# Up products of the last tile's last three MLP chunks in the first attention units, with the w2 splits placed by their use

## The chip, the cores and the metric

The kernel runs on one core of a Trainium2 chip. The metric is the time of one execution on the device in microseconds (us); less is better. A profile is one execution recorded by the hardware profiler: the engines are PE (matrix products; PEld are its weight loads), DVE (vector), ACT (activation), POOL (GpSimd) and SP, which here only issues DMAs.

## The reference

```python
xn = layernorm(x)                                    # x: 2048 x 640
# attention, 32 heads of 128, the last 512 rows of the caches
q = (xn @ wq) split into heads;  k, v = caches[:, -512:]
s = softmax(q @ k.T * 128**-0.5) @ v, heads joined, @ wo
# gated MLP, 640 -> 1728 -> 640
h = relu(xn @ w1 + b1) ** 2
g = silu(h @ w2 + b2)
out = x + s * g
```

All of it is fp32. Every product is made from three products of split operands: each operand is cut into a high part, rounded to the matrix unit's format, and a low part, the rest; hi*hi, hi*lo and lo*hi are summed in PSUM.

## The kernel before, in words

The 2048 rows are worked on in four tiles of 512, held transposed (features on partitions). `xT{t}_0` and `xT{t}_1` are the high and low part of tile t's normalized rows. The 1728 columns of w1 make 14 chunks f (13 of 128 columns and one of 64, which stands at place 3).

*First stage, the MLP of tiles 0 to 2.* For each chunk an up product (`up`, tile `ph`: 5 row chunks x 3 products, then relu with bias on ACT, square on POOL, split into hi and lo on ACT and DVE), and one step later a down product (`down`, tiles `py`, 5 output chunks x 3 products). The splits of w1 and w2 are made in tile 0 and kept in SBUF as `w1s`, `w2s`: chunks below `FA` = 11 in a pool on the right, which is closed early so that the attention's pool `ep` can take the room, the last three (11, 12, 13) in a pool on the left. `spill` copies each tile's `xT` to DRAM (`xT_d`) on POOL's DMA queue, for the attention to read later as `ax`; the last tile's copy, two of 1280 KB, is issued at the end of tile 2's MLP. The gated output `g` goes to DRAM as `g_d`.

*Second stage, attention.* There are 128 units (half of the tiles, group of two heads, tile, head), planned at a spacing `PERIOD` of 12.4 us. In unit i PE makes the scores `s` of unit i (12 products), q of unit i + 2 (`pq`, 15 products, in one of two PSUM banks `qr0`, `qr1`), the product with v of unit i - 1 (`o`, 12 products) and, from unit 3 on, the output products `r` (also in `qr0`/`qr1`). Between s and the next s lies a chain: DVE takes the maximum (`rdm`, `r1m`), PE turns it (`ptm`), DVE makes a row (`rowm`), SP sends the row to DRAM and back as a broadcast (`m_d`, then `bm`), DVE subtracts it from s (`e`), which frees the PSUM of s for the unit after. ACT takes the exponential and the high part (`pt`), POOL the low part (`pt`) and the sum of the two halves (`su`); the sum takes a like way (`rds`, `r1s`, `pts`, `rows`, `s_d`, `bs`) to normalize o into `ot`.

*Third stage, the tail.* The MLP of the last tile (`LATE` = 3) was not made in the first stage. Its up products (`late_up`, tile `lu`, `lu{f}`) and down products (`late_down`, tiles `ly`) are placed in and behind the last units, chunk by chunk: weights are loaded again (`late_load`: `l1r`, `l2r`) and split again (`late_prep`: `l1w`, `l2w`), then relu, square and split (`lr`, `lh`). Raw w2 chunks of even f share one buffer (`rawo`), those of odd f take one of the three `e` buffers; the split w2 rotates through four. The order on PE is u4, d0, five r groups, then d1 u5 d2 u6 ... d9 u13 d10, and at the end the down products of chunks 11, 12 and 13, one output chunk at a time, with `late_gate` behind each. During the tail SP also loads `fx`, `fg` and stores the tile before it (`finish`).

*What sets the order.* Every instruction of the attention stage and of the tail is put into a list with a planned time by `at(when, f, *args)`; the list is sorted by that time and the instructions are issued in that order. Each engine, and SP's DMA queue, works strictly in that order; the planned time only sorts. Waits for data and buffers are added by the framework. The helpers record all engines' instructions of these stages on one line, L72 of the kernel before.

Of the kernel before, what the change touches and what calls it, by code (L numbers as in the profile page):

```python
# [8 lines left out]
F32 = mybir.dt.float32  # L9
# [11 lines left out]
def kernel(  # L21
# [63 lines left out]
    g_d = [dpool.tile([P, DC, NT], F32, name=f"g_d{t}") for t in range(LATE)]  # L85
    s_d = [dpool.tile([P, DC, NT], F32, name=f"s_d{t}") for t in range(NTILE // 2)]

    def raw(ap):
# [21 lines left out]
    for f, (f0, n) in enumerate(chunks):  # L110
        wp = wpa if f < FA else wpb
        if n < P:
            w1s.append([wp.tile([P, DC, 2 * n], F32R, name=f"w1s{f}")])
        else:
            w1s.append([wp.tile([P, DC, n], F32R, name=f"w1s{f}_{i}") for i in range(2)])
        w2s.append([wp.tile([P, D], F32R, name=f"w2s{f}_{i}") for i in range(2)])
# [10 lines left out]
    def ln_stats(t):  # L127
# [25 lines left out]
        if t == 0:  # L153
# [49 lines left out]

    def spill(t, xs):
        for i in range(2):
            pool.dma_start(xT_d[t][i], raw(xs[i]))
# [110 lines left out]
    def mlp_step(n):  # L317
        if n < len(steps):
# [230 lines left out]
    def o_hi(i):  # L549
        OT[i] = [  # L550
            ap.tile([P, NT], F32R, tag=f"o{k}", name=f"ot{i}_{k}", bufs=2 * G)
            for k in range(2)
        ]
        act.activation(OT[i][0], PO[i], AF.Copy)
# [18 lines left out]
    def r_acc(i, d):  # L573
        hf, g, t, h = units[i]
        pr = PRS.pop((i, d))
        if g == 0:
            if d == 0:
                ACC[hf, t] = ap.tile(
                    [P, DC, NT], F32, tag="acc", name=f"acc{hf}_{t}", bufs=TPH
                )  # L580
# [92 lines left out]

    def late_relu(f):
        n = chunks[f][1]
        ph = LPH.pop(f)
        r = LR[f] = raw_tile("kv"[f % 2], f"lr{f}")[:n, :]
        bias = b1_sb[:n, f : f + 1]
# [100 lines left out]
    def at(when, f, *a):  # L779
        plan.append((max(when, 0.0), len(plan), f, a))  # L780
# [35 lines left out]
    for i in range(NU):  # L816
# [98 lines left out]
    for f, u in sorted(UP_AT.items()):  # L915
# [5 lines left out]
        relu, square, split = STEPS_AT.get(f, (u + 3.5, u + 4.3, u + 5.7))  # L921
        at(relu, late_relu, f)
# [59 lines left out]
```

## Time and profile before

| | |
|---|---|
| median of 3 runs | 2028.66 us (2024.62 to 2028.72) |
| the profiled execution | 2028.13 us, span of the instructions 2026.4 us |
| PE busy | 1989.4 us, 98% |
| DVE, POOL, ACT busy | 1537.6, 1375.9, 988.5 us |
| DMA | 218.15 MB, mean 108 GB/s |
| start of unit 0's s products | 307.0 us from the span's start |
| start of unit 4's s products | 357.2 us |
| last s products | 1905.7 us |

A row of a timeline gives start, duration, engine, line, operation, output and inputs, count, and in brackets the idle time before it and what ended that. A row of groups gives the summed busy time and the mean in ns of one instruction, then the idle time before them. A row of the chain of waits gives start, length and what that step was. Share of busy time is a mean over stages; the stages are read one by one.

### The profile page before, as it was taken

To read this page: it belongs to the slowest core of one execution; us is meant where nothing else is said; L and a number is where in the kernel's file an instruction comes from. 1 tells how busy PE (TensorE), PEld (TensorE's weight loads), DVE (VectorE), ACT (ScalarE), POOL (GpSimd) and SP (SyncE) were. 2 spreads that over 40 slices of the span, in tenths; PEclk is the share of its full clock that TensorE was granted. 3 is DMA by queue.
4 is the path that set the end of the run, shared out by engine and by line. 5 is a ranking of instruction groups with operands and counts; after the bars stand their busy time and mean duration, and the time that the engine had idled before them with its cause. 6 is when DMAs were issued, how large, how long until landed. Compare 5 with 4: busy or idle time off the path is not lost.

```text
span 2026.4 us, 24994 instructions
## 1 busy us (share of the span) xinstructions
PE 1989.4 (98%) x8832; PEld 1611.2 (80%) x8832; DVE 1537.6 (76%) x2252; ACT 988.5 (49%) x1269; POOL 1375.9 (68%) x749
## 2 busy tenths in 40 slices
PE   7999998999999999999999999999999999999998
PEld 6788885888888788888887788888888888888887
DVE  5532236788888888888887878888888888888864
ACT  4432334655555555555554465555555555555533
POOL 1121216787777777777877777888888888877842
PEclk9999999999999999999999999999999999999999
DMA  4430444333333233223235533343333333223353
GB/s 138 129 113 28 166 175 141 89 90 89 89 89 90 88 90 89 91 93 93 94 92 164 151 89 106 110 110 113 108 120 111 114 107 115 90 89 89 109 155 98
DMA packets 126589, 218.15 MB, mean 108 GB/s; under 512 B 21270, under 2 KB 37952, under 8 KB 124928
## 3 DMA queue, kind: packets, MB, share of 16 engines
q1 hardware_dynamic: 123984, 202.12, 33.2%
q0 software_dynamic: 2480, 14.43, 1.8%
q8 instruction: 70, 1.15, 0.2%
q14 instruction: 55, 0.45, 0.1%
HBM read 193.67 MB, written 22.82 MB: 107 GB/s over the span
## 4 chain that ended last, share of the span: by engine, by line
PE 89%; DMA 7%; DVE 3%; ACT 1%; issue 0%; POOL 0%; SPq 0%; ACTq 0%; DVEq 0%; POOLq 0%
PE pq L72 20%; PE r L72 20%; PE s L72 17%; PE o L72 15%; DMA bm<-m_d 2%; PE lu L72 2%; PE py L95 2%; PE py L96 2%; PE py L94 2%; PE ph L95 2%; PE ph L94 2%; PE ph L96 2%; PE ly L72 2%; DMA w1r<-in_w_dram 2%; DMA m_d<-rowm 2%; DVE e L72 1%
## 5 line engine op out<-in xcount | busy, mean ns | idle before, releaser
L72 POOL TENSOR_TENSOR pt<-e,pt 128x1024 fp32r<-128x1024 f32 x256 | 616.6, 2409 | 296.5 <-ACT pt L72 292.3
L72 PE MATMUL r<-ot,wo 128*128 128x512 f32 x1920 | 497.0, 389 | 0.1
L72 PE MATMUL pq<-ax,wq 128*128 128x512 f32 x1920 | 473.1, 396 | 0.1
L72 ACT ACTIVATE e<-e 128x1024 f32<-128x1024 f32 x256 | 269.6, 1053 | 364.1 <-DVE e L72 340.1
L72 PEld LDWEIGHTS r<-ot,wo 128*128 128x128 f32 x1920 | 360.3, 188 | 75.4 <-DVE acc L72 0.5
L72 PEld LDWEIGHTS pq<-ax,wq 128*128 128x128 f32 x1920 | 351.1, 188 | 84.4 <-DMA ax<-xT_d 0.5
L72 PE MATMUL s<-q,wk 128*128 128x512 f32 x1536 | 374.6, 393 | 12.7 <-DVE e L72 12.4
L72 PE MATMUL o<-pt,wv 128*128 128x512 f32 x1536 | 386.2, 398 | 0.5 <-POOL pt L72 0.5
L72 DVE TRANSPOSE_TENSOR_REDUCE rdm<-s 128x32 f32<-128x1024 f32 x256 | 319.6, 1250 | 67.2 <-PE s L72 53.5
L72 PEld LDWEIGHTS s<-q,wk 128*128 128x128 f32 x1536 | 288.0, 189 | 81.2 <-DVE e L72 16.7
L72 PEld LDWEIGHTS o<-pt,wv 128*128 128x128 f32 x1536 | 278.7, 188 | 70.4 <-POOL pt L72 1.4
L72 DVE TENSOR_TENSOR e<-s,bm 128x1024 f32<-128x1024 f32 x256 | 300.0, 1213 | 32.5 <-DMA bm<-m_d 28.6
L72 POOL TENSOR_TENSOR su<-e,e 128x1024 f32<-128x1024 f32 x128 | 308.1, 2407 | 0.0
L72 ACT ACTIVATE pt<-e 128x1024 fp32r<-128x1024 f32 x256 | 271.9, 1062 | 7.8
L72 DVE TENSOR_TENSOR acc<-r,acc 128x512 f32<-128x512 f32 x300 | 202.4, 675 | 2.3 <-PE r L72 2.3
L227 POOL TENSOR_TENSOR r<-r 128x512 f32<-128x512 f32 (+1 forms) x42 | 44.1, 1049 | 233.1 <-ACT r L268 214.0
L72 ACT ACTIVATE ot<-o 128x512 fp32r<-128x512 f32 x128 | 76.8, 600 | 230.0 <-DVE o L72 230.0
L72 DVE TRANSPOSE_TENSOR_REDUCE rds<-su 128x32 f32<-128x1024 f32 x128 | 158.5, 1239 | 8.7 <-POOL su L72 7.2
L72 ACT ACTIVATE q<-pq 128x512 fp32r<-128x512 f32 x128 | 76.7, 600 | 172.8 <-PE pq L72 172.8
L72 DVE TENSOR_TENSOR ot<-o,ot 128x512 fp32r<-128x512 f32 x128 | 88.4, 690 | 31.0 <-ACT ot L72 31.0
L229 DVE TENSOR_TENSOR h<-r,h 128x512 fp32r<-128x512 f32 (+1 forms) x42 | 29.0, 690 | 104.6 <-ACT h L228 104.5
L72 POOL TENSOR_TENSOR wq<-qr,wq 128x640 fp32r<-128x640 f32 x62 | 97.3, 1570 | 6.0 <-ACT wq L72 5.4
(117 smaller groups left out, 2156.7 us busy)
## 6 DMA issues: line engine op xcount, KB each, us to landing
bm<-m_d SPq DMA_DIRECT2D x128, 256.0 KB, 3.2
bs<-s_d SPq DMA_DIRECT2D x128, 256.0 KB, 4.0
qr<-in_wq_dram SPq DMA_DIRECT2D x64, 320.0 KB, 4.4
or<-in_wo_dram SPq DMA_DIRECT2D x64, 320.0 KB, 4.4
kr<-in_kT_dram SPq DMA_DIRECT2D x64, 256.0 KB, 4.5
vr<-in_v_dram SPq DMA_DIRECT2D x64, 256.0 KB, 4.3
xT_d<-xT POOLq DMA_DIRECT2D x8, 1280.0 KB, 8.5
xb<-in_x_dram SPq DMA_DIRECT2D x16, 320.0 KB, 3.6
```

The lines of the kernel that those rows point to most:

```text
L72: ins = method(*args, **kwargs)
L94: nc.tensor.matmul(ps, ah, bh, start=first and i == 0, stop=False)
L95: nc.tensor.matmul(ps, ah, bl, start=False, stop=False)
L96: nc.tensor.matmul(ps, al, bh, start=False, stop=last and i == n - 1)
L227: nc.gpsimd.tensor_tensor(r, r, r, op=ALU.mult)
L229: nc.vector.tensor_tensor(lo, r, raw(hi), op=ALU.subtract)
```

## The change

The up products, relu and square of the last tile's chunks 11, 12 and 13 are made in attention units 0, 1 and 2 (`early_up`, in bank `qr0`, behind the unit's q products), with the split w1 that the first stage still holds and with `xT3` from SBUF. Their split products are stored to DRAM one unit later (`early_split`, `h_d`, two stores each on SP) and loaded in the tail (`late_h`). The w1 chunks 11 to 13 are no longer loaded and split a second time. For this the split w1 of chunks 10 to 13, and `xT` of the odd tiles, lie in a pool `keep` that stays open: the same buffers later hold `ot` and `acc`. The raw tiles of v and of wo move from `ep` to the pool `at`.

The last tile's copy to DRAM is issued in unit 1, between POOL's work there, in place of the end of tile 2's MLP. In the tail the order becomes ... d6 u10 d7 d8 d9 d10 and the end; each w2 chunk's split is placed nine planned us before its use, or when its buffer is free. The loads of `ax` for the second half are spread as five in a planned period, 0.9 apart, in place of four, 1.2 apart. In units 0 and 1 the transpose of the sum stands ahead of the o products.

```diff
+    keep = ctx.enter_context(tc.tile_pool(name="keep", bufs=1))
...
+            if f < FA - 1:
+                w1p = [wp.tile([P, DC, n], F32R, name=f"w1s{f}_{i}") for i in range(2)]
+            else:
+                two = keep.tile([P, 2, D], F32R, tag="ot", name=f"w1s{f}", bufs=4)
...
         xs = [
-            xp.tile([P, DC, NT], F32R, tag=f"xT{i}", name=f"xT{t}_{i}") for i in range(2)
+            keep.tile([P, DC, NT], F32R, tag="acc", name=f"xT{t}_{i}", bufs=2)
+            if t % 2
+            else xp.tile([P, DC, NT], F32R, tag=f"xT{i}", name=f"xT{t}_{i}", bufs=1)
...
-            if t == LATE - 1 and f in (3, FC - 1):
-                spill(t + (f != 3), XS[t + (f != 3)])
+            if t == LATE - 1 and f == 3:
+                spill(t, XS[t])
...
-        pool_of = pools["ep"] if kind in "qkvo" else ap
+        pool_of = pools["ep"] if kind in "qk" else ap
...
+    def early_up(f, k, c):
+        if c == 0:
+            LPH[f] = bank(f"eu{f}", k)
+        w, xs = w1s[f], XS[LATE]
+        triple(LPH[f], (w[0][:, c, :], w[1][:, c, :]), (xs[0][:, c, :], xs[1][:, c, :]), c == 0, c == DC - 1)
+
+    def early_split(f):
+        r = LR.pop(f)
+        hi, lo = (
+            ap.tile([P, NT], F32R, tag=f"raw{n}", name=f"eh{f}_{n}", bufs=1) for n in "xg"
+        )
+        act.activation(hi, r, AF.Copy)
+        dve.tensor_tensor(lo, r, raw(hi), op=ALU.subtract)
+        for k, h in enumerate((hi, lo)):
+            sp.dma_start(h_d[f][:, k, :], raw(h))
+
+    def late_h(f):
+        kind, bufs = ("wv", G) if f < FC - 1 else ("q", AHEAD + 1)
+        LH[f] = pair(kind, [P, NT], f"lh{f}", bufs)
+        for k in range(2):
+            sp.dma_start(raw(LH[f][k]), h_d[f][:, k, :])
...
-                k, n = divmod(2 * c + i, 4)
-                at(w + k * PERIOD + 1.2 * n, load_xT, 1, t, i, slice(c, c + 1))
+                k, n = divmod(2 * c + i, DC)
+                at(w + k * PERIOD + 0.9 * n, load_xT, 1, t, i, slice(c, c + 1))
...
-        on(PERIOD + 9.2, turn, i, "s")
+        on(PERIOD + (8.45 if i < FC - FA - 1 else 9.2), turn, i, "s")
...
-    for f in range(5, FC):
+    for f in range(5, FA):
         order += [f"d{f - 4}", f"u{f}"]
-    order += ["d10", "e"]
+    order += [f"d{f}" for f in range(FA - 4, FA)] + ["e"]
...
+    PREP2 = {}
     for f, u in sorted(DOWN_AT.items()):
-        DOWN_AT[f] = min(u - 5.0, now - 6.0 - 5.0 * (FC - 1 - f))
-        at(DOWN_AT[f - 2] + 0.9 if f > 1 else u - 12.0, late_load, 2, f)
-        at(DOWN_AT[f], late_prep, 2, f)
+        free = DOWN_AT[f - 4] + STEP["d"] + 0.2 if f > 3 else 0.0
+        PREP2[f] = max(free, u - 9.0) if f else u - 5.0
+        at(PREP2[f - 2] + 0.9 if f > 1 else u - 12.0, late_load, 2, f)
+        at(PREP2[f], late_prep, 2, f)
+        if f >= FA:
+            at(now - 8.0 - 4.0 * (FC - f), late_h, f)
+    for k, f in enumerate(range(FA, FC)):
+        t0 = k * PERIOD
+        for c in range(DC):
+            at(t0 + 8.0 + 0.1 * c, early_up, f, 0, c)
+        at(t0 + 10.6, late_relu, f, "s")
+        at(t0 + 12.0, late_square, f)
+        at(t0 + PERIOD + 7.6, early_split, f)
+    for i in range(2):
+        at(PERIOD + 10.6 + 1.4 * i, spill, LATE, XS[LATE], (i,))
```

More of the change, by code (lines that the diff above doesn't have):

```diff
@@ L86 @@
     s_d = [dpool.tile([P, DC, NT], F32, name=f"s_d{t}") for t in range(NTILE // 2)]
+    h_d = {f: dpool.tile([P, 2, NT], F32, name=f"h_d{f}") for f in range(FC - 3, FC)}
     def raw(ap):
@@ L114 @@
         else:
-            w1s.append([wp.tile([P, DC, n], F32R, name=f"w1s{f}_{i}") for i in range(2)])
+            if f < FA - 1:
+                w1p = [wp.tile([P, DC, n], F32R, name=f"w1s{f}_{i}") for i in range(2)]
+            else:
+                two = keep.tile([P, 2, D], F32R, tag="ot", name=f"w1s{f}", bufs=4)
+                w1p = [two[:, i, :].rearrange("p (c n) -> p c n", n=n) for i in range(2)]
+            w1s.append(w1p)
         w2s.append([wp.tile([P, D], F32R, name=f"w2s{f}_{i}") for i in range(2)])
@@ L163, in ln_stats @@
         xs = [
-            xp.tile([P, DC, NT], F32R, tag=f"xT{i}", name=f"xT{t}_{i}") for i in range(2)
+            keep.tile([P, DC, NT], F32R, tag="acc", name=f"xT{t}_{i}", bufs=2)
+            if t % 2
+            else xp.tile([P, DC, NT], F32R, tag=f"xT{i}", name=f"xT{t}_{i}", bufs=1)
+            for i in range(2)
         ]
@@ L202, in ln_first, with spill @@
         return xs
-    def spill(t, xs):
-        for i in range(2):
+    def spill(t, xs, tiles=range(2)):
+        for i in tiles:
             pool.dma_start(xT_d[t][i], raw(xs[i]))
@@ L549, in o_hi @@
     def o_hi(i):
[L550 to L553, printed above, removed]
+        two = keep.tile([P, 2, D], F32R, tag="ot", name=f"ot{i}", bufs=2 * G)
+        OT[i] = [two[:, k, :NT] for k in range(2)]
         act.activation(OT[i][0], PO[i], AF.Copy)
@@ L577, in r_acc @@
             if d == 0:
-                ACC[hf, t] = ap.tile(
+                ACC[hf, t] = keep.tile(
                     [P, DC, NT], F32, tag="acc", name=f"acc{hf}_{t}", bufs=TPH
@@ L921 @@
         relu, square, split = STEPS_AT.get(f, (u + 3.5, u + 4.3, u + 5.7))
-        at(relu, late_relu, f)
+        at(relu, late_relu, f, "kv"[f % 2])
         at(square, late_square, f)
         at(split, late_split, f)
+    PREP2 = {}
     for f, u in sorted(DOWN_AT.items()):
-        DOWN_AT[f] = min(u - 5.0, now - 6.0 - 5.0 * (FC - 1 - f))
-        at(DOWN_AT[f - 2] + 0.9 if f > 1 else u - 12.0, late_load, 2, f)
-        at(DOWN_AT[f], late_prep, 2, f)
+        free = DOWN_AT[f - 4] + STEP["d"] + 0.2 if f > 3 else 0.0
[13 more added lines that the diff above has]
+        at(PERIOD + 10.6 + 1.4 * i, spill, LATE, XS[LATE], (i,))
     at(z + 2.0, late_x)
```

11 lines of the change are left out of this document (9 added, 2 removed).

## The prediction, made before the changed kernel ran

> **What bounds the kernel now.** I read the page's totals first, then the busy time in stretches cut at the starts of the units, then TensorE's (PE's) timeline in the first units and the chain of waits in the tail. All of them are of the one profiled execution.
>
> ```profile
> span 2026.4 us, 24994 instructions
> ...
> PE 1989.4 (98%) x8832; PEld 1611.2 (80%) x8832; DVE 1537.6 (76%) x2252; ACT 988.5 (49%) x1269; POOL 1375.9 (68%) x749
> ```
> ```profile
> 280.00:307.00 27.00, 27.00 (x121) 22.36 (x120) 12.85 (x19) 12.32 (x19) 6.73 (x10) 1.00 0.88 336
> 307.00:319.52 12.52, 6.44 (x29) 4.71 (x28) 5.67 (x8) 2.42 (x5) 2.90 (x3) 0.95 0.68 239
> 319.52:333.32 13.80, 12.19 (x42) 9.09 (x42) 8.06 (x12) 7.72 (x10) 9.99 (x6) 0.80 0.16 44
> 333.32:344.88 11.56, 10.05 (x42) 7.15 (x42) 9.15 (x14) 6.46 (x8) 10.77 (x6) 1.00 0.34 98
> 344.88:357.21 12.33, 11.41 (x48) 8.62 (x49) 10.18 (x14) 7.48 (x9) 10.42 (x6) 1.00 0.32 94
> 357.21:1905.72 1548.51, 1542.47 (x6890) 1248.22 (x6889) 1311.16 (x1896) 806.91 (x1005) 1234.73 (x626) 1.00 0.34 102
> ...
> 1943.00:2006.37 63.37, 63.25 (x279) 52.27 (x279) 30.36 (x34) 22.85 (x35) 24.13 (x17) 1.00 0.48 143
> ```
> Columns: stretch, its length, then busy time of PE, PE's weight loads, DVE, ACT, POOL, then the granted clock. PE is full everywhere but in the four stretches between 307.00 and 357.21: these are attention units 0 to 3, into which the r products come only at the end, and there PE is busy 40.1 of 50.2 us. In the tail (1943 to 2006) it is idle 0.12 us. So work taken out of the tail is worth its full PE time, if work put into the first units lands in holes. The change moves exactly such work, and does not alter how much of it there is.
>
> Where the holes are:
> ```profile
> 306.84 2.88 PE L72 MATMUL s<-q,wk 128*128 128x512 f32 x12
> ...
> 312.51 0.27 PE L72 MATMUL ptm<-ident,r1m 128*16 128x128 f32 x1 [1.43 <-issue]
> 312.54 2.33 PE L72 MATMUL pq<-ax,wq 128*128 128x512 f32 x9
> 319.52 5.46 PE L72 MATMUL s<-q,wk 128*128 128x512 f32 x12 [4.66 <-DVE e L72]
> ...
> 333.32 3.06 PE L72 MATMUL s<-q,wk 128*128 128x512 f32 x12 [1.40 <-DVE e L72]
> ...
> 344.88 3.03 PE L72 MATMUL s<-q,wk 128*128 128x512 f32 x12 [0.76 <-DVE e L72]
> ...
> 354.38 1.45 PE L72 MATMUL o<-pt,wv 128*128 128x512 f32 x5 [0.26 <-POOL pt L72]
> ```
> Each unit's s products wait for the unit before: maximum, row through DRAM, broadcast, subtraction on DVE. In unit 0 that leaves PE idle for 4.66 us in one piece, and the next s group takes 5.46 us where 333.32 shows 3.06: the granted clock is 0.80 over that stretch.
>
> **The change part by part.** *Tail: three up groups less.*
> ```profile
> 1985.97 3.40 PE ly L72 x15
> 1989.37 3.40 PE lu L72 x15
> ...
> 2002.97 3.40 PE lu L72 x15
> 2006.37 5.45 PE ly L72 x24
> 2011.85 0.70 ACT lsg L72
> ```
> The up groups of chunks 11 to 13 are three pieces `lu` of 15 products, the first and the last of them shown, back to back with the down groups `ly`: 3 x 3.40 = **10.20 us off the path**. The end behind them (the last `ly`, sigmoid, DVE, stores) is unchanged.
>
> What could take it back is the supply of w2: chunks 7 to 10 now follow each other every 3.4 us, not 6.8.
> ```profile
> DMA to landing us min/median/max: 2.9/5.5/6.7
> ```
> ```profile
> L72 DVE TENSOR_TENSOR l2w<-l2r,l2w 128x640 fp32r<-128x640 f32 x14 | 15.2, 1086 | 6.5 <-ACT l2w L72 6.5
> L72 ACT ACTIVATE l2w<-l2r 128x640 fp32r<-128x640 f32 x14 | 10.2, 731 | 6.3 <-DMA l2r<-in_w_dram 5.6 <-PE ly L72 0.7
> ```
> ```profile
> 1978.38 0.69 DVE L72 TENSOR_TENSOR acc<-acc,fg 128x512 f32<-128x512 f32 x1 [2.35 <-DMA fg<-g_d]
> ```
> (The first row is the landing time of all w2 loads, `l2r`.) In the old trace's clock chunk 7's down group still starts at 1985.97, and 8, 9, 10 and the end follow at 1989.4, 1992.8, 1996.2 and 1999.6. Even chunks share one raw buffer, so their loads go one after another. DVE is held by the `fg` load until 1979.1, then does one more step of 0.7 and the splits of 7 and 8 (1.1 each): 8 is ready at 1982. Load 10: 0.4 for the issue (estimate), 5.5, 0.7, 1.1, ready at 1989.7, needed 1996.2. Load 12: ready at 1997.4, needed one group of three products into the end, at 2000.3. 2.9 us to spare; with both loads at the longest landing, 6.7, still 0.5. The odd chunks rotate through three buffers and are not in this. The six loads of the stored products stand on SP ahead of load 12 and are due only at 1999.6. I take nothing for the supply, and up to 1.5 in the range.
>
> *Units 0 to 2: the three groups come in.* The build's order puts each behind its unit's q products, ahead of the o products. Unit 0: q ends at 312.54 + 2.33 = 314.87, the new group at 318.3, and s of unit 1 is released at 319.52 as before. Cost 0; the hole left is 1.26 us, shorter than the 1.40 at 333.32 behind which s took 3.06.
>
> Unit 1: s 3.06, not 5.46; then q 3.40, new group 3.40, o 12/15 x 3.40 = 2.72, two transposes and a short wait for the maximum 0.5 (estimate): 13.1, against 13.80 before. From the end of s to the next s the old chain took 333.32 - 324.98 = 8.34, so its release would be at 330.9 and PE, at 332.6, is the later one: 0.7 us gained.
>
> Unit 2: s 2.72, q 3.40, new 3.40, o 2.72, 0.5: PE could start unit 3 at 345.4. DVE may be later:
> ```profile
> 333.17 1.57 POOL L72 TENSOR_TENSOR wo<-or,wo 128x640 fp32r<-128x640 f32 x1
> 335.53 2.40 POOL L72 TENSOR_TENSOR pt<-e,pt 128x1024 fp32r<-128x1024 f32 x1 [0.79 <-ACT pt L72]
> ...
> 347.21 2.40 POOL L72 TENSOR_TENSOR pt<-e,pt 128x1024 fp32r<-128x1024 f32 x1 [1.82 <-ACT pt L72]
> ```
> ```profile
> 340.31 1.25 DVE L72 TRANSPOSE_TENSOR_REDUCE rds<-su 128x32 f32<-128x1024 f32 x1 [0.40 <-POOL su L72]
> ...
> 342.60 0.34 DVE L72 RECIPROCAL rows<-rows 16x32 f32<-16x32 f32 x1
> ```
> ```profile
> L72 POOL DMA_DIRECT2D xT_d<-xT x8 | 4.4, 550 | 0.0
> L72 POOL TENSOR_TENSOR lr<-lr 128x512 f32<-128x512 f32 x13 | 14.8, 1139 | 29.9 <-ACT lr L72 29.9
> L72 DVE TENSOR_TENSOR lh<-lr,lh 128x512 fp32r<-128x512 f32 x13 | 11.7, 901 | 16.6 <-ACT lh L72 16.5
> ```
> On POOL two copy issues (0.55 each) and a square (1.14) now stand between `wo` and `pt`, 2.2 us. With the earlier ACT (s not slow) `pt` starts at about 336.2, 0.7 late, and the sum `su` ends at 341.0. Behind it DVE does what took 340.31 to 342.94, and the early split's subtraction (0.9): 344.5, then the subtraction that releases s (1.2). Unit 3 starts at 345.7, against 344.88. In unit 3 POOL's third square fits into the 1.82 of idle time, and its `pt` still ends the wait for o, so the length stays 12.3. **Sum of the first units: +0.8** (0 if the DVE steps overlap better, +1.5 if every estimate is short).
>
> *The last tile's copy* (two of 1280 KB, POOL's queue) leaves the stretch before 307, where PE was full: no gain. It now travels while unit 2's row goes out and back.
> ```profile
> 327.33 1.33 DMA m_d<-rowm
> 328.67 3.34 DMA bm<-m_d
> ...
> 1092.18 3.37 DMA m_d<-rowm
> 1095.57 4.42 DMA bm<-m_d
> ```
> ```profile
> 1101.29 3.02 PE L72 MATMUL s<-q,wk 128*128 128x512 f32 x12 [2.10 <-DVE e L72]
> ```
> The nearest rows are at 1092, behind six loads of 256 KB on the same queue: 7.8 in place of 4.7, +3.1. Unit 2's broadcast would land at about 342.8 and DVE is ready at 344.5, so 1.7 of it is covered: 0 to +1.4. The Trainium skill ("DMA: Bandwidth & Descriptors", Queues, rings and completion order) says that a DMA engine takes turns between queue rows packet by packet. By that the row's own queue would not stand behind the copy, and the cost would be 0; no run here shows a row beside a POOL copy. From the rows I take **+0.4**, nearer the covered end because the copy is on another queue.
>
> *Second-half loads, five in a unit, where the built order had 4, 4, 6, 4 and 2.* The one behind six cost 2.10 (above), and all PE idle from 357 to 1905 is 6.0. Between these: -1 to +1.5; I take **+0.2**.
>
> *Costed at nothing:* `vr0`, `or0` now wait for the MLP's buffers (about 304), covered until the first o products at 329; the six stores of the early splits on SP stand ahead of the sum's row, which DVE finishes after them; three relus and copies on ACT, 49% busy; the transpose of units 0 and 1, now ahead of the o products, comes behind a new group that ends no earlier than its input; the moved buffers add no instruction, and their first users come long after the last readers.
>
> **Sum:** -10.2 + 0.8 + 0.4 + 0.2 = -8.8. The execution took 2028.13 with a span of 2026.4; that gives 2019.3. The median of the runs shown, 2028.66, stands 0.5 above it and their lowest, 2024.62, 3.5 below. What can be told from no change is 0.2%, 4 us.
>
> **The rivals.**
> 1. *The copy collides more than once:* it also holds the sum's row of unit 1 and the loads of unit 3, at 3.1 each with no cover: about +4 on the forecast, 2023. Against: 2.6 MB at the 336 GB/s of 280:307 is 8 us, less than a unit. For: those rows are on the critical chain in these units.
> 2. *The first units hide nothing:* each new group delays the next s by its full length, because POOL or DVE already sets the pace there (POOL is busy 10.77 of 11.56 in unit 2). +10.2 eats the gain: 2028.5, no change. Against: 4.66 of idle PE in unit 0 alone, and the slow 5.46.
> 3. *Slower: the w2 supply becomes the tail's bound.* Place: chunks 8, 10, 12 with their one raw buffer. It decides from a landing of about 7.0 us on; beyond that each us costs two. At a landing of 12.5 the end is 11 us late: 2030. The longest seen is 6.7, and the stretch has fewer loads than before, against it; the tighter spacing and the h loads are for it.
> 4. *It doesn't do what it says:* the first new group held by its PSUM bank or by buffers, so that s of unit 1 starts late. q of unit 1 left that bank before 312: very unlikely.
>
> **How the numbers follow.** Forecast 0.70; rival 1 0.12; rival 2 0.10; rival 3 0.06; rival 4 0.02, taken as slower. The low end, 2015.0, is the forecast with 0.8 and 0.4 at zero, the second-half loads at -1 (2016.9) and half of the 3.5 us by which a single run fell below. The high end, 2024.5, is the forecast with every cost at its bound (+1.5, +1.4, +1.5, supply +1.5, thus 2023.8), and takes rival 1 in. Faster by over 0.2% (below 2024.6): forecast and rival 1, 0.82. Within: rival 2, 0.10. Slower: 0.08.
>
> **What would show it.** In the new profile: `eu` directly behind the q products in units 0 to 2; no 5.46 at 319.5 and a granted clock of 1.00 there; the fourth s group after 307 within 2 us of 357.2; `ly` back to back, with no `lu` between the last four whole groups; the PE sum unchanged. Wrong would be: an idle PE of more than 1 us between 1985 and the end's sigmoid, a broadcast above 5 us near 340, or units 1 and 2 longer than 14 us.

## The result, and the profile after

The changed kernel is slower. Its median is 2030.29 us over 20 runs (2027.7 to 2033.96), that of the kernel before 2024.82 us over 20 runs (2022.43 to 2028.74): a ratio of 1.0026, 95% interval 1.0019 to 1.0033, thus about +5.3 us (the medians themselves differ by 5.5). The prediction was -8.8 us from a profiled execution that took 2028.13 us, which by these runs lies 3.3 us above its own kernel's median. The profiled execution of the changed kernel took 2027.7 us and is the fastest of its twenty. So the two profiles alone differ by -0.4 us, and the places have to be read stage by stage.

The page of the changed kernel, first lines:
```profile
span 2025.9 us, 25005 instructions
...
PE 1989.3 (98%) x8832; PEld 1612.1 (80%) x8832; DVE 1536.9 (76%) x2252; ACT 985.6 (49%) x1266; POOL 1370.6 (68%) x746
```
PE's work is the same (1989.4 before), as the prediction said. Next, busy time by stretch, cut at the starts of the s groups of units 0 to 4 and 127 and at the first of the back-to-back `ly` groups; the columns are stretch, length, then busy time of PE, PE's weight loads, DVE, ACT, POOL, granted clock, DMA share, GB/s. After:
```profile
305.19:316.63 11.44, 9.98 (x45) 7.69 (x43) 5.79 (x8) 3.42 (x6) 3.45 (x4) 1.00 0.51 185
316.63:329.75 13.12, 12.75 (x56) 10.02 (x57) 9.16 (x13) 8.64 (x12) 10.69 (x6) 1.00 0.31 92
329.75:346.52 16.77, 13.11 (x58) 9.95 (x57) 13.22 (x15) 7.66 (x11) 14.90 (x11) 1.00 0.73 254
346.52:359.42 12.90, 12.53 (x48) 9.51 (x48) 9.65 (x15) 6.99 (x10) 10.01 (x5) 0.87 0.41 126
359.42:1908.59 1549.17, 1543.27 (x6888) 1249.68 (x6889) 1310.05 (x1896) 807.07 (x1005) 1234.39 (x626) 1.00 0.33 102
1908.59:1955.15 46.56, 42.63 (x179) 33.62 (x178) 30.94 (x43) 19.69 (x29) 23.57 (x13) 0.96 0.38 115
1955.15:2011.00 55.85, 55.85 (x248) 46.27 (x247) 24.53 (x28) 19.36 (x30) 15.40 (x11) 1.00 0.57 172
```
The stretch of before that answers to the sixth of these:
```profile
1905.56:1946.14 40.58, 40.46 (x179) 32.54 (x178) 31.19 (x42) 19.75 (x28) 25.59 (x14) 1.00 0.43 133
```
Three readings. Unit 1 is what was forecast, 13.1 us; unit 0, whose length the prediction left as it was, takes 11.4 in place of 12.7. Unit 2 takes 16.77 us where 13.1 was forecast, with POOL busy for 14.90 of it and DVE for 13.22, about 4 us more than in the units beside it. And between the last s group and the back-to-back tail, where the prediction looked for nothing, the same 179 products take 46.56 us in place of 40.58: PE is idle for 3.9 us in place of 0.1, and the rest is a lower granted clock behind that idle time (0.80 from 1946.60 to 1955.15).

**Unit 2.** PE's timeline of the changed kernel:
```profile
311.93 3.56 PE L72 MATMUL eu<-xT,w1s 128*128 128x512 f32 x15
316.63 2.99 PE L72 MATMUL s<-q,wk 128*128 128x512 f32 x12 [1.14 <-DVE e L72]
...
329.75 2.99 PE L72 MATMUL s<-q,wk 128*128 128x512 f32 x12
...
346.52 4.61 PE L72 MATMUL s<-q,wk 128*128 128x512 f32 x12 [3.28 <-DVE e L72]
```
The new group `eu` fills unit 0's hole, the s group of 5.46 us (granted clock 0.50 while it ran) is gone, and unit 1 ends without idle time. But the hole comes back two units later: 3.28 us before unit 3's s, which then takes 4.61. The second profile of the changed kernel has the same hole, and its s group keeps the full clock, so the hole belongs to the kernel and the slow s group does not always follow:
```profile
347.12 3.02 PE L72 MATMUL s<-q,wk 128*128 128x512 f32 x12 [3.28 <-DVE e L72]
```
DVE in unit 2, first profile:
```profile
338.60 1.25 DVE L72 TRANSPOSE_TENSOR_REDUCE rds<-su 128x32 f32<-128x1024 f32 x1 [1.62 <-POOL su L72]
...
339.99 4.23 DVE L72 TENSOR_TENSOR eh_g<-lr,eh_x 128x512 fp32r<-128x512 f32 x1
344.14 0.68 DVE L72 SCALAR_TENSOR_TENSOR q<-pq,q 128x512 fp32r<-128x512 f32 x1
344.74 0.27 DVE L72 TENSOR_REDUCE rows<-pts 16x32 f32<-16x128 f32 x1
345.04 0.34 DVE L72 RECIPROCAL rows<-rows 16x32 f32<-16x32 f32 x1
345.31 2.28 DVE L72 TENSOR_TENSOR e<-s,bm 128x1024 f32<-128x1024 f32 x2
```
and POOL beside it:
```profile
338.52 2.40 POOL L72 TENSOR_TENSOR pt<-e,pt 128x1024 fp32r<-128x1024 f32 x1
340.86 1.56 POOL L72 TENSOR_TENSOR wq<-qr,wq 128x640 fp32r<-128x640 f32 x1
342.38 1.27 POOL L72 TENSOR_TENSOR wk<-kr,wk 128x512 fp32r<-128x512 f32 x1
```
The early split's subtraction `eh_g`, both of whose inputs lie in SBUF, takes 4.23 us. Its shortest, in another unit, is 0.68; the second profile shows 4.23 in unit 2 again. It begins inside POOL's `pt` and ends 0.57 us after POOL's `wk`, so its 4.23 us cover the rest of one POOL instruction and the whole of the two behind it; that it stood still meanwhile is read from this timing. The four DVE steps behind it, the release of s last, moved with it. The Trainium skill (SBUF — State Buffer, "SBUF: two separate sides") says that a DVE instruction with two SBUF inputs and a GpSimd instruction that reads SBUF exclude each other, the later one waiting for the whole of the other. The rows agree, and add that a waiting DVE can be passed by POOL's next instructions.

A second wait lies under the first. SP's issues after, the maximum's row out (`m_d`) and its broadcast back (`bm`, issued when the row has landed):
```profile
335.84 0.32 SPq L72 DMA_DIRECT2D m_d<-rowm  x1
340.93 0.33 SPq L72 DMA_DIRECT2D bm<-m_d  x1
```
and before:
```profile
338.77 0.32 SPq L72 DMA_DIRECT2D m_d<-rowm  x1
340.09 0.33 SPq L72 DMA_DIRECT2D bm<-m_d  x1
```
The row of 2 KB takes 5.1 us beside the last tile's copy (issued at 331.59 and 333.19), 1.3 without it. The broadcast then lands 3.8 us after its issue, at about 344.7, only 0.6 before DVE turns to `e`.

**Ahead of the tail.** ACT after, then PE after:
```profile
1945.33 0.74 ACT L72 ACTIVATE l2w<-l2r 128x640 fp32r<-128x640 f32 x1 [6.90 <-DMA l2r<-in_w_dram]
1945.97 0.58 ACT L72 ACTIVATE ot<-o 128x512 fp32r<-128x512 f32 x1
```
```profile
1946.61 0.51 PE L72 MATMUL r<-ot,wo 128*128 128x512 f32 x1 [3.46 <-ACT ot L72]
1947.58 7.73 PE L72 MATMUL r<-ot,wo 128*128 128x512 f32 x26 [0.47 <-DVE ot L72]
```
and ACT before, then PE before:
```profile
1938.02 0.60 ACT L72 ACTIVATE ot<-o 128x512 fp32r<-128x512 f32 x1 [3.00 <-DVE o L72]
...
1940.99 0.74 ACT L72 ACTIVATE l2w<-l2r 128x640 fp32r<-128x640 f32 x1 [1.85 <-DMA l2r<-in_w_dram]
```
```profile
1938.89 7.42 PE L72 MATMUL r<-ot,wo 128*128 128x512 f32 x30
```
The `l2w` is the splitting of w2 chunk 1. It is planned nine ahead of its use now, no longer five, which puts it in front of the last unit's `ot` in ACT's order and in DVE's. Its load has not landed, ACT stands still for 6.90 us, and `ot`, whose input `o` was ready at 1942.5 (1941.81 + 0.70 on DVE), waits behind it. The output products r wait for `ot`. In the kernel before, `ot` runs first and the wait for the load comes behind it, where PE has the thirty r products to do.

**The tail** does what was forecast:
```profile
1994.82 23.96 PE L72 MATMUL ly<-lh,l2w 128*128 128x512 f32 x105
```
These are the four groups of 15 of chunks 7 to 10 and the 45 products of the end, back to back, with no `lu` between them and no idle PE.

### The profile page after: what moved, and what is told of

The parts are those of the page before. It is cut to its first block, busy times and chain, and to the rows that moved or that the text cites. A ratio compares the mean times of both kernels' runs of the same rounds, so it can differ in the third digit from the quotient of the medians.

```text
span 2025.9 us, 25005 instructions
## 1 busy us (share of the span) xinstructions
PE 1989.3 (98%) x8832; PEld 1612.1 (80%) x8832; DVE 1536.9 (76%) x2252; ACT 985.6 (49%) x1266; POOL 1370.6 (68%) x746
## 4 chain that ended last, share of the span: by engine, by line
PE 90%; DMA 4%; DVE 2%; POOL 1%; ACT 1%; issue 1%; SPq 0%; POOLq 0%; DVEq 0%
PE pq L72 21%; PE r L72 21%; PE s L72 17%; PE o L72 16%; DMA w1r<-in_w_dram 2%; PE py L96 2%; PE py L97 2%; PE py L95 2%; PE ph L95 2%; PE ph L97 2%; PE ph L96 2%; PE ly L72 2%; PE lu L72 1%; DMA bm<-m_d 1%; DMA m_d<-rowm 1%; PE ptm L72 1%
## 5 line engine op out<-in xcount | busy, mean ns | idle before, releaser
L72 PE MATMUL s<-q,wk 128*128 128x512 f32 x1536 | 375.3, 394 | 10.3 <-DVE e L72 10.2
```

The source lines that it names most:

```text
L72: ins = method(*args, **kwargs)
```

## The experiments

The table puts all profiles side by side. It is worked out from PE's timeline of each: the start of unit 0's s, the lengths from s to s of units 0 to 3 and their sum, from unit 4's s to unit 127's, from there to the first of the back-to-back `ly`, and from there to the span's end. The last column is the ratio of the times to those of the kernel before that was measured beside it, with its 95% interval; it can differ from the ratio of the two medians by some 0.0003.

```
kernel                       s0     units 0, 1, 2, 3            sum    middle   ahead  behind  ratio
before                       306.8  12.68 13.80 11.56 12.17   50.2   1548.5   40.6   80.3
before, second profile       306.5  14.48 13.65 11.30 12.13   51.6   1545.7   40.5   80.2
after                        305.2  11.44 13.12 16.77 12.90   54.2   1549.2   46.6   70.8   1.0026 [1.0019, 1.0033]
after, second profile        305.8  11.59 13.16 16.57 12.18   53.5   1549.2   48.3   70.8
e1  w2 chunk 1 as before     306.0  11.48 13.13 16.70 13.18   54.5   1544.9   41.5   70.7   0.9993 [0.9984, 1.0002]
e2  subtraction later        306.7  11.30 13.79 16.76 13.87   55.7   1546.1   47.6   70.1   1.0021 [1.0012, 1.0030]
e3  e1 + e2                  306.8  11.49 13.80 16.85 13.87   56.0   1546.7   41.6   70.1   1.0006 [0.9997, 1.0014]
e4  subtraction on POOL      307.9  11.48 13.14 15.66 12.06   52.3   1545.3   47.2   70.8   1.0008 [0.9999, 1.0016]
e5  before, w2 chunk 1 early 307.1  13.51 13.22 11.34 12.11   50.2   1544.3   44.9   80.2   1.0024 [1.0015, 1.0033]
e7  e1 + e4                  308.5  11.76 13.14 15.53 12.01   52.4   1549.9   42.3   70.8   0.9990 [0.9981, 0.9998]
e8  e1 + e4 + copy back      305.5  13.15 14.72 13.04 11.26   52.2   1547.0   42.4   70.8   0.9979 [0.9971, 0.9988]
e9  e1 + copy back           308.1  13.54 15.61 13.02 11.75   53.9   1548.6   42.4   70.7   0.9988 [0.9979, 0.9997]
e10 before, new ax spacing   306.8  13.60 12.89 11.28 12.13   49.9   1545.9   40.1   80.2   1.0000 [0.9991, 1.0009]
e11 e8 + old ax spacing      307.3  13.47 14.70 13.03 11.35   52.6   1549.9   42.6   70.3   0.9986 [0.9977, 0.9995]
e12 e7, copy in unit 4       307.6  11.43 13.15 13.06 12.54   50.2   1554.9   42.7   70.9   1.0016 [1.0008, 1.0025]
e13 e7, copy in ten pieces   306.2  11.53 13.16 14.48 14.66   53.8   1550.1   42.5   70.0   0.9994 [0.9985, 1.0002]
e14 after, old ax spacing    305.1  11.34 13.19 16.80 13.69   55.0   1548.3   48.2   70.3   1.0021 [1.0011, 1.0031]
```

**The second w2 chunk's split (e1).**
```diff
-        PREP2[f] = max(free, u - 9.0) if f else u - 5.0
+        PREP2[f] = max(free, u - 9.0) if f > 1 else u - 5.0
```
The load of chunk 3, whose planned time hangs on this split, moves with it here and in e5.

> One edit on the changed kernel: the splitting of the tail's second w2 chunk (l2w1) is placed 5 ahead of its use again, as in the kernel before, so that it stands behind the last unit's ot127 on ACT and DVE. Theory A (l2w1, waiting for its load, held ot127 and with it the output products r): the stretch from the last unit's s group to the first of the back-to-back ly groups falls from 46.6 us to about 41 to 42, and the median lies 4 to 6 us under the changed kernel's 2030.3, at 2024.5 to 2026.5, within 0.1% of the kernel before. Theory B (that stretch is longer because three up groups no longer fill it, or because the last tile's activations come later): it stays at 46 us and the median within 1 us of 2030. The first units stay at 54 us in both.

The stretch falls to 41.5 us and the ratio from 1.0026 to 0.9993: theory A, at the upper end of its size or above it (0.0033 is 6.7 us). PE there:
```profile
1940.23 3.47 PE L72 MATMUL r<-ot,wo 128*128 128x512 f32 x14 [0.22 <-DVE ot L72]
```
The 3.46 us of idle PE ahead of r is gone; 0.22 is left there.

**The same step alone on the kernel before (e5).**
```diff
-        DOWN_AT[f] = min(u - 5.0, now - 6.0 - 5.0 * (FC - 1 - f))
+        DOWN_AT[f] = min(u - (9.0 if f == 1 else 5.0), now - 6.0 - 5.0 * (FC - 1 - f))
```


> The kernel before with one part of the change alone: its second w2 chunk's split is placed 9 ahead of use in place of 5, so that l2w1 stands ahead of ot127 on ACT, as in the changed kernel. Theory A (the split ahead of ot127 costs the changed kernel its 6 us there by itself): the stretch from the last unit's s to the first back-to-back ly grows from 40.6 us to 45 to 47, and the median by 4 to 6 us, ratio 1.002 to 1.003. Theory B (it costs only together with the shorter tail): less than 1 us.

Ratio 1.0024, +4.9 us: the edit costs nearly what the whole change cost, with the rest of the kernel untouched. PE:
```profile
1937.79 0.51 PE L72 MATMUL r<-ot,wo 128*128 128x512 f32 x1 [2.15 <-ACT ot L72]
1938.76 7.80 PE L72 MATMUL r<-ot,wo 128*128 128x512 f32 x26 [0.47 <-DVE ot L72]
```
The same pair of waits as in the changed kernel; ACT stands 5.59 us for the load. Theory A; the mechanism needs nothing else of the change.

**The early split's subtraction moved behind the shift (e2), and with e1 (e3).** ACT's rounding and DVE's subtraction become two steps; the relu and square behind them are placed later.
```diff
-        at(t0 + 10.6, late_relu, f, "s")
-        at(t0 + 12.0, late_square, f)
-        at(t0 + PERIOD + 7.6, early_split, f)
+        at(t0 + 15.0, late_relu, f, "s")
+        at(t0 + 18.7, late_square, f)
+        at(t0 + PERIOD + 7.6, early_hi, f)
+        at(t0 + PERIOD + 11.65, early_lo, f)
```


> One edit on the changed kernel: the early split is cut in two. ACT's rounding stays where it is; DVE's subtraction (both operands in SBUF) and the two stores of h come 4 us later, behind the next unit's shift, where GpSimd is idle ahead of its pt; the relu and square that follow are placed 4 to 7 us later so that their buffer order stays. Theory A (the subtraction waits until GpSimd pauses, 4.23 us in unit 2 in place of 0.7, and the release of unit 3's s stands behind it): subtraction at most 1.6 us in each of the three units, unit 2 back to 13 to 13.5 us from 16.8, the four units 50 to 51 us from 54.1, the median 3 to 4 us under the changed kernel's 2030.3, at about 2026.5. Theory B (the last tile's copy delays the maximum's row or its broadcast): unit 2 stays at 16 us or more with the subtraction short, median 2030. Theory C (GpSimd's added squares and copy issues make pt late): the same as B, with PE waiting for pt.

> Both edits together on the changed kernel: the second w2 chunk's split 5 ahead of its use, and the early split's subtraction behind the shift. If the two causes are right and independent, the gains add: 7 to 10 us under the changed kernel's 2030.3, thus 2020 to 2023, 2 to 5 us under the kernel before (ratio 0.9975 to 0.999). If the profiled execution of the changed kernel, which lies 2.6 us under its own median, hides a third loss, the sum falls short by it: 2024 to 2025, the same as before. If the two share one cause (the last tile's copy), the sum is that of the larger alone, about 2025.

Theory A of e2 fell. The subtraction is short in all three units (0.67 to 0.68 us), and unit 2 still takes 16.76. DVE and ACT in e2:
```profile
332.74 0.67 DVE L72 TENSOR_TENSOR eh_g<-lr,eh_x 128x512 fp32r<-128x512 f32 x1
...
345.19 0.69 DVE L72 SCALAR_TENSOR_TENSOR q<-pq,q 128x512 fp32r<-128x512 f32 x1 [3.02 <-ACT q L72]
...
347.22 2.36 DVE L72 TENSOR_TENSOR e<-s,bm 128x1024 f32<-128x1024 f32 x2 [0.78 <-DMA bm<-m_d]
```
```profile
344.04 0.63 ACT L72 ACTIVATE eh_x<-lr 128x512 fp32r<-128x512 f32 x1 [6.00 <-POOL lr L72]
```
Two things hold it. The edit itself made a new wait: POOL's square now comes behind both `pt`, ACT's rounding waits 6.00 us for it, and q's shift behind that. And with DVE ready again, the broadcast `bm` is last, by 0.78 us: the copy (theory B). e3 shows the same unit 2 and, at 1.0006, misses the 0.9975 to 0.999 that two independent gains would have given; against e2 the first experiment's edit is worth 0.0015, against the changed kernel 0.0033, with intervals of about 0.0009 to each side of each ratio.

**The subtraction on POOL (e4).**
```diff
-        dve.tensor_tensor(lo, r, raw(hi), op=ALU.subtract)
+        pool.tensor_tensor(lo, r, raw(hi), op=ALU.subtract)
```


> One edit on the changed kernel: the early split's subtraction is made on GpSimd in place of DVE, in the same place of the order. If DVE's wait for GpSimd is the cause in unit 2, it is gone, at the price of one more GpSimd step of about 1.1 us in each of units 1, 2 and 3, before or among its weight splits: DVE's release of unit 3's s comes 3 to 4 us earlier, unit 2 is 13 to 14 us, the median 1 to 4 us under the changed kernel's 2030.3. If GpSimd's load in these units is itself the bound, pt is late by about 1 us per unit instead, and the median stays within 1 us of 2030. If the copy's traffic is the cause, nothing changes: unit 2 at 16 us or more.

Unit 2 falls by 1.1 us, not by 3 to 4. Unit 3, no longer at a lower clock, is 0.8 shorter than in the changed kernel's first profile and 0.1 shorter than in its second, where the lower clock is absent too. The ratio falls by 0.0018, 3.6 us, of which the first units explain 1.2 to 1.9. DVE in unit 2:
```profile
346.94 2.36 DVE L72 TENSOR_TENSOR e<-s,bm 128x1024 f32<-128x1024 f32 x2 [2.21 <-DMA bm<-m_d]
```
DVE now stands idle 2.21 us for the broadcast alone. So two waits of nearly the same length had stood side by side in the changed kernel, and taking one away uncovers the other.

**The copy back at the end of the MLP, with e1 and e4 (e8) and with e1 alone (e9).**
```diff
-            if t == LATE - 1 and f == 3:
-                spill(t, XS[t])
+            if t == LATE - 1 and f in (3, FC - 1):
+                spill(t + (f != 3), XS[t + (f != 3)])
...
-    for i in range(2):
-        at(PERIOD + 10.6 + 1.4 * i, spill, LATE, XS[LATE], (i,))
```


> The changed kernel with three edits: the second w2 chunk's split 5 ahead of its use, the early split's subtraction on GpSimd, and the last tile's copy to DRAM back at the end of the MLP of the tile before. Theory A (two waits were stacked in unit 2, DVE's subtraction held by GpSimd and, behind it, the row that lands after 5.1 us in place of 1.3 because of the copy): with both gone the row takes 1.3 to 2 us, unit 2 is 13 to 13.5 us, the first four units 50 to 50.5 us, the tail stays at 70.5 to 71 and the stretch ahead of it at 41.5; 4 us under the first experiment's ratio of 0.9993, thus 0.997 to 0.998, and 2016.5 to 2019 against a kernel before of 2022.8. Theory B (GpSimd's load is the bound of unit 2): unit 2 stays at 15.5 us and the ratio at 0.9985 to 0.999, the sum of the first and the fourth experiment alone.

> As the kernel of the same call with three edits, but with the early split's subtraction left on DVE: the second w2 chunk's split 5 ahead of its use, and the copy back at the end of the MLP. It tells the copy from the subtraction. If the subtraction's wait for GpSimd bounds unit 2 by itself, it still takes 3 to 4 us there, and unit 2 goes only from 16.8 to 15 to 15.6 us (two copy issues of 0.6 less ahead of GpSimd's pt); ratio 0.9985. If the copy alone was the cause, unit 2 is 13 to 13.5 us and the ratio 0.997 to 0.998 as with all three edits.

Unit 2 is 13.0 us in both, and its row takes 1.3 us again: the copy was the wait below. e8's ratio is the one that theory A gave, e9's is 0.0003 from the other theory's though its unit 2 is as short. But units 0 to 3 together are not at the 50 to 50.5 us that were expected: the sum is 52.2 in e8, no better than with the copy in unit 2 (52.4, e7), because units 0 and 1 grow by 1.4 and 1.6. In all seven profiles with the copy at the end of the MLP (before twice, e5, e8 to e11) unit 0 takes 12.7 to 14.5 us; in the ten with the copy elsewhere 11.3 to 11.8. What the copy is in the way of there is seen first in unit 0's row, SP in e8:
```profile
310.62 0.32 SPq L72 DMA_DIRECT2D m_d<-rowm  x1
313.15 0.33 SPq L72 DMA_DIRECT2D bm<-m_d  x1
```
The row takes 2.5 us here, 3.0 in e9 and e11, and 1.4 in the changed kernel. DVE waits 3.51 us for the broadcast where it waited 1.80, and PE's hole in front of unit 1's s grows from 1.14 to 2.84 us; behind it that s takes 4.58 in place of 2.99, which is unit 1's growth. In the kernel before, unit 0's row is not late (1.4); in its second profile and in e5 it is the maximum that waits, for the stores of the MLP's last results, which stand on the copy's queue and took 6.6 us to land (median) in before's first profile and 4.3 in the changed kernel's. DVE in the second profile of before:
```profile
311.24 2.38 DVE L72 TRANSPOSE_TENSOR_REDUCE rdm<-s 128x32 f32<-128x1024 f32 x2 [3.27 <-DMA g_d<-sgl]
```
e8 is the fastest version tried, 0.9979, about 4.3 us under the kernel before and 9.6 under the changed one; its interval overlaps those of e7, e9 and e11.

In e9, where nothing was done about the subtraction, it takes 1.41 us in unit 2, not 4.23. DVE, then POOL, in e9:
```profile
344.96 1.41 DVE L72 TENSOR_TENSOR eh_g<-lr,eh_x 128x512 fp32r<-128x512 f32 x1
```
```profile
343.41 2.41 POOL L72 TENSOR_TENSOR pt<-e,pt 128x1024 fp32r<-128x1024 f32 x1
345.78 2.02 POOL L72 TENSOR_TENSOR wq<-qr,wq 128x640 fp32r<-128x640 f32 x1
```
Here DVE got through when `pt` ended, and it was POOL's `wq` that became longer, 2.02 for 1.56. Which engine goes first isn't fixed; what decides it, no run here shows. So no run has a subtraction of 4.23 us without the copy: that it would hold unit 2 alone is read from the changed kernel's rows, where `e` follows the DVE steps without idle time.

**The copy's place, with e1 and e4: where the change put it (e7), in unit 4 (e12), in ten pieces (e13).** e12 writes `3 * PERIOD` for `PERIOD` in the copy's planned time; e13 is
```diff
-        at(PERIOD + 10.6 + 1.4 * i, spill, LATE, XS[LATE], (i,))
+    for k, w in enumerate((10.6, 18.7, 23.0, 24.0, 31.1, 35.4, 36.4, 43.5, 47.8, 48.8)):
+        at(w, spill_part, *divmod(k, DC))
```


> The changed kernel with the second w2 chunk's split 5 ahead of its use and the early split's subtraction on GpSimd; the last tile's copy stays where the change put it. Against the kernel with the copy back at the MLP's end it prices the copy's new place. From the stages of the runs before: units 0 to 3 at 11.5, 13.1, 15.7 and 12.1 us, sum 52.3, with the row of unit 2 at 5.1 us, against 13.2, 14.7, 13.0 and 11.3, sum 52.2, with the copy back. Theory A (the copy only moves its collision from units 0 and 1 to unit 2): ratio 0.9975 to 0.9985, the same as with it back. Theory B (the copy's new place is the larger loss): ratio 0.999 or more.

> As the kernel with the second w2 chunk's split 5 ahead of its use and the subtraction on GpSimd, but with the last tile's copy two units later still, in unit 4, where the first r products give PE work beside a late row. Theory A (the copy costs where PE has nothing else): unit 2 falls from 15.7 to about 13 us, units 0 to 3 to 49 to 50 us, and the row that the copy delays costs at most 1 to 2 us in unit 4; ratio 0.996 to 0.9975. Theory B (the late row costs its 3.8 us wherever it stands): the loss moves to unit 4 and the ratio stays at 0.998.

> As the kernel with the second w2 chunk's split 5 ahead of its use and the subtraction on GpSimd, but with the last tile's copy cut into ten pieces of 256 KB that are issued one or two at a time over units 0 to 4. If a row waits only for what is in flight when it is issued, each row is late by at most one or two pieces (0.8 us each at the 330 GB/s that the copy reached) in place of 3.8: unit 2 at 13 to 14 us, units 0 to 3 at 50 to 51.5 us, ratio 0.9965 to 0.9975. If GpSimd's ten issues of 0.6 us cost more than the row gains, unit 2 stays above 15 us and the ratio at 0.998.

e7's ratio, 0.9990, stands at the edge of theory B, the stages at theory A: the sums of the first units are equal within 0.3 us, and the intervals of e7 and e8 (0.9979) overlap. By the stages the copy's new place moves its collision rather than making or sparing one; that it costs some 2 us more by the medians is neither shown nor excluded. In e12 both theories missed: units 0 to 3 are the best of all with the new groups, 50.2 us, and the kernel is slower, 1.0016. PE in unit 4:
```profile
365.43 1.66 PE L72 MATMUL pq<-ax,wq 128*128 128x512 f32 x6 [3.37 <-ACT acc L72]
```
The first accumulator `acc` takes the buffer from which the copy still reads, and PE waits for ACT, which waits 6.47 us for the copy. So e12 says nothing clear on the price of a late row in unit 4. In e13, expected at 0.9965 to 0.9975 and measured at 0.9994, unit 2 falls to 14.48 and unit 3 grows to 14.66: the late rows are spread, not spared. SP in unit 2 of e13:
```profile
336.60 0.33 SPq L72 DMA_DIRECT2D m_d<-rowm  x1
338.77 0.33 SPq L72 DMA_DIRECT2D bm<-m_d  x1
```
A row beside one or two pieces takes 2.2 us, between 1.3 and 5.1.

**What the stages leave open: the ax loads' spacing (e10, e14, e11) and repeated profiles.** e10 gives the kernel before the new spacing (five in a unit, 0.9 apart), e14 gives the changed kernel the old one (four, 1.2 apart), e11 gives it to e8.

> The kernel before with the change's spacing of the second half's ax loads alone (five in a unit, 0.9 apart, where it had four, 1.2 apart). Theory C (the new spacing delays rows in the middle of the kernel; the stages of the profiles leave some 2 to 4 us of the changed kernel's median unexplained): ratio 1.001 to 1.002, and longer waits of s for DVE between 1067 and 1200 us. Theory D (the two profiles compared are one high and one low draw, and the spacing costs nothing): ratio 1.000 within its interval, the stretch from the fifth s to the last unit's s at 1545 to 1548 us as in all kernels.

> One edit on the changed kernel: the spacing of the second half's ax loads is the old one, four in a unit and 1.2 apart. Theory C (five loads ahead of a unit's row cost 2 to 4 us on the changed kernel, though they cost nothing on the kernel before): the four units from about 1059 on take 54.5 to 55.5 us in place of 57.7, the middle stretch 1546 to 1547, and the ratio falls from 1.0026 to 1.001 to 1.0015. Theory D (the units around 1059 vary by themselves): ratio 1.002 to 1.003, and their sum anywhere from 54 to 58.

> The kernel with three edits (the second w2 chunk's split 5 ahead of its use, the subtraction on GpSimd, the copy back at the MLP's end; ratio 0.9979) with the old spacing of the second half's ax loads as well. Theory C: 2 to 3 us lower, ratio 0.9965 to 0.997, the four units from about 1059 on at 54.5 to 55.5 us in place of 58.2. Theory D: ratio 0.9975 to 0.9985.

> The changed kernel once more, for a second profile. The first lies 2.6 us under the median of its twenty runs. If that is scatter spread over the long middle stretch, this one shows 54 us for units 0 to 3, 46.5 ahead of the first back-to-back ly and 70.7 behind it again, and a middle stretch of 1545 to 1550 us. If instead the units 0 to 3 vary from run to run, their sum differs here by over 1 us.

> The kernel before once more, for a second profile. Its first lies 3.3 us above the median of its runs. Expected if that is scatter of the middle stretch: units 0 to 3 at 50 us, 40 to 40.6 ahead of the first back-to-back ly, 80.2 behind it, and a middle stretch of 1544 to 1547 us, thus a span of 2021 to 2024.

None of the three ratios moves outside its interval (1.0000; 1.0021 for 1.0026; 0.9986 for 0.9979): theory D, at the resolution of these runs. The four units from 1059 us on, in which these loads are issued, do differ. From s to s they take 57.7 and 57.6 us in the two profiles of the changed kernel, 55.8 in e14, 54.5, 53.2 and 55.4 in before twice and e5, 55.0 in e10; but 53.7 in e1 and 57.2 in e8, whose loads are placed the same, and 56.2 in e11 with the old spacing, so they vary by some 3 us by themselves. Over all seventeen profiles the mean is 55.6 with the new spacing and 55.0 with the old. The repeats say the same of the whole: the first units differ by 0.7 us (after) and 1.4 (before), the middle by 0.0 and 2.8, the stretch ahead of the tail by 1.7 and 0.1, the tail by 0.1 at most. Two things missed what was expected of the repeats: the first units of before took 51.6 us for 50, and the stretch ahead of the tail of the changed kernel 48.3 for 46.5.

## Why the prediction was wrong

From the means of two profiles each, after less before: start of unit 0 -1.2, units 0 to 3 +3.0, middle +2.0, ahead of the back-to-back `ly` +6.9, behind it -9.5; sum +1.3. (The start of unit 0 lies between 305.1 and 308.5 us over the versions and is not counted for the change.) The prediction's terms, one by one:

- *Tail, three up groups less, -10.2.* Right: -9.5 in the mean, and every version with the change shows it (70.0 to 70.9 for 80.2). The 0.7 that is missing lies in the last stores: from the last DVE step to the end of the span it is 3.9 us where it was 3.2.
- *w2 supply, nothing.* This is the step that failed. It was worked out for the chunks from 7 on, where the spacing becomes tighter, and it held there. The edit to the splits' lead, however, applies to all chunks, and the first one that it moved was chunk 1, past the last unit's `ot` on ACT and DVE, in front of a load that had not landed. The prediction asked when the loads of the chunks at the end would land; it did not ask which step stands behind chunk 1's split on ACT and who waits for that step. It cost 6.9 us by the stages, 4.9 (e5) to 6.7 (e1) by the ratios. With the smaller figure the forecast of -8.8 becomes -3.9, with the larger one -2.1. Rival 3 had the right subject, w2, but the wrong place and a landing time as its condition; the load of chunk 1 took 6.2 us to land, within the 6.7 that the prediction allowed. That rival 3's time, 2030, is the one measured is luck. None of the signs that the prediction listed lay in this stretch.
- *Units 0 and 1.* Right in what they do: the group behind q, a hole of 1.14 us where 1.26 was to remain, no slow s behind it, and unit 1 at the 13.1 that was forecast. Unit 0 is better than forecast, 11.4 us for 12.7.
- *Unit 2, +0.8 with the DVE order, and the copy, +0.4.* Both mis-sized; this is the second, smaller failure. The subtraction was taken at 0.9 from the mean of `lh` and took 4.23: the mean held rows from 0.68 to 2.55 us, and here POOL has three instructions in a row. The copy was taken as 3.1 on row and broadcast together; the row alone took 3.8 more. Counted from unit 2's s, DVE's turn to release the next s came after 15.6 us by the subtraction (345.31) and would have come after about 15.0 by the broadcast (344.7); the prediction had 11.9 and 10.2 (344.5 and 342.8, with unit 2's s at 332.6). So either one moves it by over 3 us, and together they move it hardly further. In unit lengths, the copy alone is worth 2.6 us (e4's 15.66 against e8's 13.04) and the subtraction on top of it 1.1. Unit 2 became 16.77, and in one profile of the two unit 3's s lost another 1.6 at a lower clock. Unit 2 above 14 us is one of the signs of being wrong that the prediction had named. Rival 1 priced the copy at +4, but by other rows, unit 1's sum and unit 3's loads.
- *The copy leaves the stretch before 307, "no gain".* Wrong: with the new group in both, unit 0 takes 13.2 to 13.5 us with the copy ahead of it (e8, e9, e11) and 11.3 to 11.8 without, and unit 1 14.7 to 15.6 in place of 13.1 to 13.8. It is a gain that unit 2 gives back, which is why the copy's place hardly shows in the ratios.
- *Second-half loads, +0.2.* Not contradicted; not resolved either: 55.6 for 55.0 us in four units that vary by 3.
- *The base.* The sum was made against an execution of 2028.13 us; the median of 20 runs is 2024.82. The forecast time is 3.3 too high for that alone; the forecast difference isn't touched.

With the two causes taken back (e8) the kernel is 4.3 us under the one before, by medians, about half of the 8.8 that were forecast. Its first units are 1.3 us above before's mean; that the prediction's 0.8 and 0.4 add up to nearly this is chance, since they were made for the copy's other place. Another 1.9 are still lost ahead of the tail, where the prediction had nothing. Its stages sum to -7.6 against the mean of before's two profiles; the 3.3 between that and the medians is of the size by which before's first profile stands above its own median. Left open: of the +5.3 of the changed kernel its stages show +1.3. Both of its profiles lie under its median (2027.7 and 2029.29 for 2030.29) and both of before above (2028.13 and 2026.24 for 2024.82), which makes 4.1 between them; whether a place in the middle stretch is also slower in most runs of the changed kernel, two profiles of each don't tell.

## What to carry to other kernels

When one constant moves a family of prefetch steps, list for every member what it now passes on its in-order engine: the dangerous one is not where the schedule gets tight but where a step that waits for a load is put in front of a short step on the critical chain. Price a DVE instruction with two SBUF inputs by what POOL does at that moment, not by its mean over the kernel. None of the places tried for the large copy was free here, beside a chain that goes through DRAM or before a buffer's next use: before moving one, look at what it delays where it is and what it will delay there, and expect two waits of like length to hide each other.

## What the runs showed of the hardware that was not expected

- A DVE subtraction with both inputs in SBUF, 0.68 us at its shortest, took 4.23 us beside three POOL instructions in a row; in e9 it got in between two of them and POOL's was the longer, 2.02 for 1.56.
- A row of 2 KB on SP's queue took 5.1 us beside 2.6 MB on POOL's queue, 2.2 beside pieces of it, 1.3 alone. The Trainium skill (DMA: Bandwidth & Descriptors, Queues, rings and completion order) has each DMA engine take turns between queues packet by packet. The prediction noted that by this rule the row would cost 0, and took 0.4 for itself; the measured 3.8 us decides against that reading of the rule.
- Idle time alone doesn't tell whether the clock falls. Two rows of the changed kernel, in the middle stretch:
```profile
1076.47 4.60 PE L72 MATMUL s<-q,wk 128*128 128x512 f32 x12 [2.17 <-DVE e L72]
...
1106.22 3.02 PE L72 MATMUL s<-q,wk 128*128 128x512 f32 x12 [2.84 <-DVE e L72]
```
  The shorter hole is followed by the slow s, and the two profiles of the changed kernel have the same 3.28 us before unit 3's s, one with and one without it. Over the seventeen profiles no s group of 12 products took more than 3.06 us after a hole of up to 1.79 us, all three behind holes of 3.49 us and more took 4.96 or longer, and between 1.84 and 3.31 us both are found. The Trainium skill (TensorE: Matmul & The Clock Gate, "What's actually happening") speaks of an idle window of about 3.4 us that runs freely. The place of a hole in such a window may decide between equal holes, which no run here shows; but the clock fell behind holes of 1.84 us (e5) and 2.17 us, both shorter than a whole window, so the stated length doesn't hold here.
